# Two routed layers behind attention: the usual numbers of visits in line, wider first products, empty row groups not sent

## The chip, the cores and the metric

One core of one Trainium2 chip. The metric is the device time of one execution in microseconds (us), as the median of three runs. The engines are named as in the profile: PE (TensorE matmul) and PEld (its weight loads), DVE (VectorE), ACT (ScalarE), POOL (GpSimd), SP (SyncE, which issues most transfers).

## The reference

Attention with random features, then two layers with eight experts each. A token goes to the one expert with the largest logit; layer 0 keeps at most 576 tokens of an expert, layer 1 keeps all, and its logits have a bias that depends on the token's modality.

```python
# layer 0 (cap = 576); x: 2304 x 512, w1: 8 x 512 x 1024, w2: 8 x 1024 x 512
expert_idx = np.argmax(x @ w_gate, axis=1)
...
h = np.maximum(np.einsum('ecd,edf->ecf', disp, w1), 0.0)
y = np.einsum('ecf,efd->ecd', h, w2)
...
# layer 1
logits = x @ w_gate + modality_bias[modality_id]
e_idx = np.argmax(logits, axis=1)
...
    h = np.maximum(x[mask] @ w1[e], 0.0)
    out[mask] = gate_w[mask, None] * (h @ w2[e])
```

## The kernel before

The attention fills the first 255 us or so and isn't touched. Each layer is then worked off in visits. A visit takes up to 512 tokens of one expert, as four blocks of 128 rows:

- `fetch` (POOL) brings the rows `xrow` by four indirect DMAs; it is issued one or two visits ahead.
- `turn` transposes a block on PE (`pt<-ident,xrow`); ACT writes the upper part `xTh`, VectorE the rest `xTl`.
- `one` makes an eighth of the hidden layer: 12 matmuls (`pa<-xTh,wh`, `pa<-xTl,wh`, `pa<-xTh,wl`), with as many columns as the visit was built for; eight of them, 96 matmuls, make the first products.
- `keep` writes `hTh` (ACT) and `hTl` (VectorE). `piece` splits 512 columns of weights into `wh` (ACT) and `wl` (VectorE for the even pieces, POOL for the odd ones).
- `two` makes the second products, 24 matmuls for 128 columns or 128 tokens. In layer 1 it does so only for blocks below the built size.
- `out` (ACT) writes the result `y`. In layer 1 `put` (POOL) sends a block's rows to their places in the output by an indirect DMA, four in each visit, whether the block holds tokens or not; places outside the output are dropped.

Sizes are found at run time. `products` holds a matmul part once for each size in `BUILT`, and a nest of Ifs (L892) on PE alone takes one; they are called the arms. The number of visits is a run-time number as well. `others` and its inner `rest` write the program as a nest: visits 1 to 3 always run; then an If on the number of visits (L1221) holds one more full visit and the rest in its body, and the last visit in its Else. The bodies follow one another in line. All the Elses stand behind them, so that a layer's last visit is reached by a branch out of the line and left by another. (`final` is layer 0's last visit, which also fetches for layer 1; `last` is layer 1's.) Between the layers stands an If on the number of tokens of layer 1's first visit (L1258, L1259): with 512 of them `whole` runs, which mixes layer 0's last routing with layer 1's first visit; else a longer way. `L1.others` follows.

All of it is issued in written order on each engine: `in_order` ties each instruction to the one before it on its engine. Most rows of the profile therefore have the line of that helper, L55, or L53 for the first instruction of a block.

```python
                    with tc.If(self.visits > v + 1, preferred_fallthrough_block=True) as c:
                        self.visit(v)
                        rest(v + 1)
                    self.arm = arm
                    with c.Else():
                        self.visit(v, ("final", "last")[l])
```

Of the kernel before, what the change touches and what calls it, by code (L numbers as in the profile page):

```python
# [20 lines left out]
N, DM, E, FF = 2304, 512, 8, 1024  # L21
XW = 524
GATE, BIAS, TOK = 512, 513, 513
NV = 12
# [9 lines left out]
)  # L34

ALWAYS = (5, 5)


class InOrder:
# [21 lines left out]
def moe_chain_kernel(ctx, tc, q, k, v, w_phi, wg1, w1a, w2a, modality, wg2, mbias, w1b, w2b, out, cap):  # L61
    nc = tc.nc
    in_order = InOrder(tc)
# [726 lines left out]
    with ExitStack() as mo:  # L790
# [46 lines left out]
        class Layer:  # L837
# [69 lines left out]

            def one(self, f, n):

                ph = bank("pa", f)  # L910
                (xh, xl), (wh, wl) = xT, (t.rearrange("p f (c k) -> p f c k", c=4) for t in wgt[0])
                for m, (c, xt, wt) in enumerate((c, xt, wt) for c in range(4) for xt, wt in ((xh, wh), (xl, wh), (xh, wl))):
                    in_order.tensor.matmul(ph[:, 0:n], lhsT=wt[:, f, c, :], rhs=xt[:, c, 0:n], start=(m == 0), stop=(m == 11))
# [25 lines left out]
            def visit(self, v, kind=None):  # L939
# [71 lines left out]
                for f in range(4, 8):  # L1011
                    self.keep(f)
                    todo.pop(0)()
                self.mine(v, b)
                if kind is None and v + 2 < NV:
                    self.select(v + 2)
                if ev is not None:
# [4 lines left out]
                for c in range(2):  # L1022
                    for _ in range(2):
                        if later:
                            later.pop(0)()
                    self.out(c, b)
                    if l == 1:
                        self.put(c, b)
                for g in steps[2]:
                    g()  # L1030
                mine = self.arm
# [10 lines left out]
                for c in range(2, 4):  # L1042
                    for _ in range(2):
                        if later:
                            later.pop(0)()
                    self.out(c, b)
                    if l == 1:
                        self.put(c, b)
                for g in steps[3]:
                    g()  # L1050
                if kind in (None, "first") and v + 2 < (ALWAYS[0] if l == 0 else NV):
# [43 lines left out]
                self.fetch(2)  # L1095
                self.put(3, 0)

            def put(self, a, b):
                in_order.gpsimd.indirect_dma_start(out=out, out_offset=bass.IndirectOffsetOnAxis(ap=tokr[b][:, a, :], axis=0),
                                                   in_=y2[:, a, 0:DM], in_offset=None, bounds_check=N - 1, oob_is_err=False)  # L1100

# [106 lines left out]
                in_order.vector.tensor_scalar_add(first[l][:, 3:4], n, -1.0)  # L1208
                self.find_arm(0)

            def others(self):

                self.registers()
                l = self.l

                def rest(v):
                    if v + 1 == NV:
                        self.visit(v, ("final", "last")[l])
                        return
                    arm = self.arm  # L1220
                    with tc.If(self.visits > v + 1, preferred_fallthrough_block=True) as c:  # L1221
                        self.visit(v)
                        rest(v + 1)
                    self.arm = arm
                    with c.Else():
                        self.visit(v, ("final", "last")[l])

                if l == 1:
                    self.find_arm(1)
# [22 lines left out]
        L0.visit(0, "first")  # L1252
        i = 4 * NV + 1
        in_order.vector.tensor_scalar(out=lastv, in0=ctl[0][:, i - 1:i], scalar1=-1, scalar2=ALWAYS[0] - 1, op0=ALU.add, op1=ALU.max)
        L0.others()


        early = nc.values_load(first[1][0:1, 2:3], min_val=0, max_val=N)  # L1258
        with tc.If(early > 511) as c:  # L1259
            L1.whole()  # L1260
        with c.Else():
            for t in L0.tail():
                t()
            for f in visit_list(1, in_order.vector):
                f()
            L1.select(0)
            L1.fetch(0)
            L1.select(1)
            for a in range(4):
                L1.turn(a)  # L1270
            L1.fetch(1)
            L1.tokens()
            L1.visit(0)
        L1.others()


_INS = ["q", "k", "v", "w_phi", "moe_w_gate", "moe_w1", "moe_w2", "moe2_modality_id", "moe2_w_gate", "moe2_modality_bias", "moe2_w1", "moe2_w2"]
# [24 lines left out]
```

## Time and profile before

| what | us |
|---|---|
| runs | 887.31, 880.38, 880.18 |
| median | 880.38 |
| profiled execution, its own time | 886.04 |
| its span in the trace | 884.3 |
| PE busy in it | 783.4 |
| POOL busy in it | 434.5 |

In a row of the timeline the first number is the start from the span's begin, the second the duration, and the brackets say how long the engine had been idle and what ended that; `issue` means that it waited for nothing that the profile shows. Ends of matmuls are modelled, so the distance between starts tells their pace. In a row of the groups the number after x is the count, then busy time and mean ns of one, then the idle time before them. Numbers of buffers are left out of names.

### The profile page before, as it was taken

The page shows a single profiled execution, that of the slowest core. Times are in us where ns is not written, and L with a number is a line of the kernel's source. Part 1 is how long each engine was busy: PE and PEld are TensorE (multiplying, and loading weights), DVE is VectorE, ACT ScalarE, POOL GpSimd, SP SyncE. Part 2 cuts the span into 40 slices and gives each one's busy share as a digit, 9 for nine tenths or more (in the row PEclk, how much of TensorE's full clock was granted, in tenths as well). Part 3 has the DMA queues.
Part 4 walks back from the last instruction along what each step waited for, and adds up shares of the span by engine and source line. Part 5 has one row for each costly group of instructions (what it writes and reads, how often), then busy time and mean ns, then how long its engine had stood idle before and what let it go on. Part 6 is the DMA issues. An engine that isn't in the chain of part 4 may idle for free. (4 is left out here: it accounts for less than half of the span.)

```text
span 884.3 us, 15256 instructions
## 1 busy us (share of the span) xinstructions
PE 783.4 (89%) x5170; PEld 681.1 (77%) x5170; DVE 517.4 (59%) x1225; ACT 421.9 (48%) x807; POOL 434.5 (49%) x544
## 2 busy tenths in 40 slices
PE   7879999999939899999998886789699999998690
PEld 5649986589829789999988885767588888898590
DVE  7866687976647337477887765948232323266530
ACT  4547865578443335445545552522343434356431
POOL 4965537755242534564655633712644444466641
PEclk9999999999968999999999987999999999996755
DMA  8747623251032443537448444402762626274420
GB/s 268 249 174 264 211 75 112 63 215 60 3 98 92 150 171 119 200 108 269 156 141 290 140 153 142 154 2 99 236 221 83 206 66 224 72 237 139 132 52 6
DMA packets 70812, 129.44 MB, mean 146 GB/s; under 512 B 16388, under 2 KB 28804, under 8 KB 70660
## 3 DMA queue, kind: packets, MB, share of 16 engines
q1 hardware_dynamic: 60852, 103.33, 34.5%
q0 software_dynamic: 7360, 21.90, 8.6%
q10 hardware_dynamic: 2448, 2.20, 0.8%
q8 instruction: 92, 1.51, 0.7%
q14 instruction: 60, 0.49, 0.2%
HBM read 94.37 MB, written 35.67 MB: 147 GB/s over the span
## 5 line engine op out<-in xcount | busy, mean ns | idle before, releaser
L55 POOL TENSOR_TENSOR wl<-raw,wh 128x512 fp32r<-128x512 f32 x114 | 148.9, 1314 | 149.8 <-ACT wh L55 146.3
L55 PE MATMUL pa<-xTh,wl 128*128 128x512 f32 (+10 forms) x480 | 165.9, 346 | 1.7 <-issue 1.7
L55 PE MATMUL pa<-xTl,wh 128*128 128x512 f32 (+10 forms) x480 | 165.6, 345 | 0.1
L55 PE MATMUL pa<-xTh,wh 128*128 128x512 f32 (+10 forms) x451 | 155.8, 345 | 0.0
L55 ACT CAST wh<-raw 128x512 fp32r<-128x512 f32 x240 | 141.8, 620 | 6.1 <-DMA raw<-in_moe_w_dram 4.7
L55 DVE SCALAR_TENSOR_TENSOR hTl<-pa,hTh 128x512 fp32r<-128x512 f32 x112 | 76.8, 689 | 111.7 <-ACT hTh L55 110.9
L55 DVE TENSOR_TENSOR wl<-raw,wh 128x512 fp32r<-128x512 f32 x121 | 110.4, 921 | 46.3 <-ACT wh L55 46.3
L55 ACT ACTIVATE hTh<-pa 128x512 fp32r<-128x512 f32 x112 | 67.1, 599 | 138.8 <-PE pa L55 136.9
L55 PEld LDWEIGHTS pa<-xTh,wl 128*128 128x128 f32 x480 | 101.8, 212 | 7.3 <-issue 2.4
L55 PEld LDWEIGHTS pa<-xTl,wh 128*128 128x128 f32 x480 | 101.8, 212 | 5.7 <-DVE xTl L55 0.4
L55 PEld LDWEIGHTS pa<-xTh,wh 128*128 128x128 f32 x451 | 95.4, 212 | 4.6
L55 POOL DMA_INDIRECT xrow<-xs,rowi x61 | 64.8, 1062 | 51.9 <-DVE n L55 15.3
L55 PE MATMUL pa<-hTh,wl 128*128 128x424 f32 (+7 forms) x256 | 81.5, 318 | 4.4 <-POOL wl L55 4.4
L55 PE MATMUL pa<-hTl,wh 128*128 128x424 f32 (+7 forms) x256 | 81.3, 318 | 0.0
L55 PE MATMUL pa<-hTh,wh 128*128 128x424 f32 (+7 forms) x240 | 76.2, 318 | 0.0
L55 POOL DMA_INDIRECT out_dram<-y,tokr x28 | 28.3, 1011 | 75.5 <-ACT y L55 36.2
L541 PE MATMUL po<-kv,e 128*128 128x65 f32 x512 | 64.2, 274 | 0.5 <-DVE rank L677 0.5
L55 PE MATMUL pa<-wl,hTh 128*128 128x512 f32 x160 | 63.4, 396 | 0.6 <-DVE wl L55 0.6
L55 DVE TENSOR_TENSOR xTl<-pt,xTh 128x512 fp32r<-128x512 f32 x60 | 38.6, 681 | 42.7 <-ACT xTh L55 42.6
L55 PE MATMUL pa<-wh,hTl 128*128 128x512 f32 x160 | 63.2, 395 | 0.0
L541 PEld LDWEIGHTS po<-kv,e 128*128 128x128 f32 x512 | 61.0, 192 | 1.5 <-issue 0.8
L55 PE MATMUL pa<-wh,hTh 128*128 128x512 f32 x151 | 59.7, 395 | 0.0
(307 smaller groups left out, 1544.8 us busy)
## 6 DMA issues: line engine op xcount, KB each, us to landing
raw<-in_moe_w_dram SPq DMA_DIRECT2D x116, 512.0 KB, 5.1
xs<-hrow SPq DMA_DIRECT2D x18, 524.0 KB, 5.9
xs<-y SPq DMA_DIRECT2D x8, 1048.0 KB, 4.3
out_dram<-hrow SPq DMA_DIRECT2D x9, 512.0 KB, 4.7
qk_sb<-in_k_dram SPq DMA_DIRECT2D x16, 256.0 KB, 3.9
v_sb<-in_v_dram SPq DMA_DIRECT2D x16, 256.0 KB, 3.9
qk_sb<-in_q_dram SPq DMA_DIRECT2D x8, 512.0 KB, 3.8
xs<-y SPq DMA_DIRECT2D x2, 1024.0 KB, 5.5
```

The costliest lines, as they stand in the source:

```text
L55: return f(*a, **kw)
L541: nc.tensor.matmul(po[:, j, :], lhsT=e[:, sg, j, :], rhs=kv[:, h, it["b2"], sg, :], start=(sg == 0), stop=(sg == 1))
```

## The change

`LINE = (8, 7)` is new: for eight visits of layer 0 and seven of layer 1 the last visit stands in line. In `rest` the If at that visit is turned round: its body is the last visit, and more visits are in its Else. Layer 1 (`second`) is written into the body behind layer 0's eighth visit, and within it `L1.others` behind `whole`. Other numbers of layer 0's visits skip that and reach a second copy of layer 1 at the program's end. `one` takes at least 208 columns. A put of a block after the first is sent only if the visit has more tokens than stand in the blocks before; POOL reads that number once in a visit. The four puts in `whole` stay as they are.

```diff
+LINE = (8, 7)
...
             def one(self, f, n):
 
+                n = max(n, 208)
...
+                if l == 1:
+                    t = ctl[1][0:1, 2 * NV + v:2 * NV + v + 1] if v > 0 else first[1][0:1, 2:3]
+                    count = in_order.gpsimd.value_load(t, min_val=0, max_val=N)
...
                     if l == 1:
-                        self.put(c, b)
+                        self.put(c, b, count)
...
-            def put(self, a, b):
+            def put(self, a, b, count=None):
+
+                if count is not None and a > 0:
+                    with tc.If(count > 128 * a, preferred_fallthrough_block=True):
+                        self.put(a, b)
+                    return
...
-            def others(self):
+            def others(self, then=lambda: None):
...
+                def last(v):
+                    self.visit(v, ("final", "last")[l])
+                    if v + 1 == LINE[l]:
+                        then()
+
+                def more(v):
+                    self.visit(v)
+                    rest(v + 1)
+
                 def rest(v):
                     if v + 1 == NV:
-                        self.visit(v, ("final", "last")[l])
+                        last(v)
                         return
                     arm = self.arm
-                    with tc.If(self.visits > v + 1, preferred_fallthrough_block=True) as c:
-                        self.visit(v)
-                        rest(v + 1)
+                    if v + 1 == LINE[l]:
+                        cond, near, far = self.visits < v + 2, last, more
+                    else:
+                        cond, near, far = self.visits > v + 1, more, last
+                    with tc.If(cond, preferred_fallthrough_block=True) as c:
+                        near(v)
                     self.arm = arm
                     with c.Else():
-                        self.visit(v, ("final", "last")[l])
+                        far(v)
...
-        L0.others()
-
-
-        early = nc.values_load(first[1][0:1, 2:3], min_val=0, max_val=N)
-        with tc.If(early > 511) as c:
-            L1.whole()
...
+        def second():
+
+
+            early = nc.values_load(first[1][0:1, 2:3], min_val=0, max_val=N)
+            with tc.If(early > 511, preferred_fallthrough_block=True) as c:
+                L1.whole()
+                L1.others()
...
+                L1.others()
+
+        L0.others(second)
+        with tc.If(L0.visits != LINE[0], preferred_fallthrough_block=False):
+            second()
```

PE before, at the end of layer 0's last visit as the eighth, an Else: `pa` is the smallest arm of its second products, `pt` and `pm` are the transposes and a placing product behind them, L1221 is the If on the number of visits, and behind the branch stands another Else.

```order
L55 MATMUL pa_3497<-hTh,wl_3505 128x208
L892 UNCONDITIONAL_BRANCH
L55 MATMUL pt_3498<-ident,xrow 128x128 x4
L55 MATMUL pt_3499<-ident,xrow 128x128 x4
L55 MATMUL pt_3498<-ident,x 128x128 x4
L55 MATMUL pt_3499<-ident,x 128x128 x4
...
L55 MATMUL pm_3500<-B,A 128x320
L1221 UNCONDITIONAL_BRANCH
L892 COMPARE_AND_BRANCH
L53 MATMUL pa_3494<-xTh,wh_3502 128x512
```

PE in the changed program, at the end of the same visit: L1281 and L1282 are the If on layer 1's first visit, and `whole` begins with the 512-wide matmul.

```order
L57 MATMUL pa_3497<-hTh,wl_3505 128x208
L894 UNCONDITIONAL_BRANCH
L57 MATMUL pt_3498<-ident,xrow 128x128 x4
L57 MATMUL pt_3499<-ident,xrow 128x128 x4
L57 MATMUL pt_3498<-ident,x 128x128 x4
L57 MATMUL pt_3499<-ident,x 128x128 x4
...
L57 MATMUL pm_3500<-B,A 128x320
L1281 TENSOR_LOAD first_242
L1282 COMPARE_AND_BRANCH
L55 MATMUL pa_3494<-xTh,wh_3502 128x512
```

In the first, an unconditional branch leads away from the visit's end to the point where layer 1 begins; in the second, layer 1 begins behind the visit, with one compare between.

PE before, where `whole` ends: `pm_3501<-x,wgp` belongs to the Else of the If on layer 1's first visit.

```order
L55 MATMUL pa_3497<-wh_3504,hTl 128x512
L55 MATMUL pt_3498<-ident,xrow 128x128 x4
L55 MATMUL pt_3499<-ident,xrow 128x128 x4
L55 TENSOR_LOAD ctl_244
L55 ISA x2
L1259 UNCONDITIONAL_BRANCH
L53 MATMUL pm_3501<-x,wgp_226 32x512
```

PE in the changed program, at the same place.

```order
L57 MATMUL pa_3497<-wh_3504,hTl 128x512
L846 TENSOR_LOAD ctl_244
L57 TENSOR_LOAD ctl_244
L57 ISA x2
L57 MATMUL pt_3498<-ident,xrow 128x128 x4
L57 MATMUL pt_3499<-ident,xrow 128x128 x4
L57 TENSOR_LOAD ctl_244
L57 ISA x2
L894 COMPARE_AND_BRANCH
L55 MATMUL pa_3494<-xTh,wh_3502 128x512
```

The branch over the Else is gone, and the next visit's first products follow the compare of their arms.

POOL before, in a visit of layer 1: `out_dram<-y,tokr` are the puts, `xrow<-xs,rowi` the fetch of a later visit.

```order
L55 DMA out_dram<-y_254,tokr_3515 2304x512
L55 TENSOR_TENSOR wl_3503<-raw_247,wh_3502 128x512
L55 DMA out_dram<-y_254,tokr_3515 2304x512
L55 COPY side<-xrow 128x12 x2
L55 TENSOR_TENSOR wl_3503<-raw_247,wh_3502 128x512
L55 DMA out_dram<-y_254,tokr_3515 2304x512
L55 TENSOR_TENSOR wl_3503<-raw_247,wh_3502 128x512
L892 UNCONDITIONAL_BRANCH
L55 DMA out_dram<-y_254,tokr_3515 2304x512
L55 DMA xrow<-xs_61,rowi 128x524 x4
```

POOL in the changed program, in such a visit, from the second put on.

```order
L1107 COMPARE_AND_BRANCH
L55 DMA out_dram<-y_254,tokr_3515 2304x512
L1107 UNCONDITIONAL_BRANCH
L1107 ISA
L1107 UNCONDITIONAL_BRANCH
L57 COPY side<-xrow 128x12 x2
L57 TENSOR_TENSOR wl_3503<-raw_247,wh_3502 128x512
L1107 COMPARE_AND_BRANCH
L55 DMA out_dram<-y_254,tokr_3515 2304x512
L1107 UNCONDITIONAL_BRANCH
```

Each put but a visit's first now stands behind a compare, and both ways end in a branch.

## Rows read from the trace of the kernel before

**Rows 1.** Groups by line and shape, from 260 us on: visits, puts, and 128-column products

```profile
L55 DVE TENSOR_SCALAR groupr<-four_f 128x4 f32<-128x4 f32 x8 | 8.0, 996 | 0.0
...
L55 DVE CAST tokr<-sdr 128x4 int32<-128x4 f32 x7 | 3.3, 467 | 5.4 <-POOL sdr L55 5.4
...
L55 POOL DMA_INDIRECT out_dram<-y,tokr x28 | 28.3, 1011 | 75.5 <-ACT y L55 36.2 <-PEq L892 11.6 <-DMA out_dram<-y,tokr 11.3
...
L55 PE MATMUL pa<-xTh,wl 128*128 128x128 f32 x64 | 25.6, 399 | 0.0
```

**Rows 2.** Timeline of PE at the places out of line, and two starts of `pt`

```profile
538.89 0.54 PE L53 MATMUL pa<-xTh,wh 128*128 128x208 f32 x1 [6.09 <-issue]
...
577.21 0.47 PE L53 MATMUL pa<-xTh,wh 128*128 128x512 f32 x1 [3.13 <-issue]
...
579.45 0.79 PE L55 MATMUL pa<-xTh,wl 128*128 128x512 f32 x1 [0.84 <-issue]
...
637.51 0.78 PE L53 MATMUL pa<-xTh,wh 128*128 128x512 f32 x1 [5.66 <-issue]
...
817.74 2.25 PE L55 MATMUL pt<-ident,xrow 128*128 128x128 f32 x8 [0.89 <-DMA xrow<-xs,rowi]
...
826.03 1.03 PE L55 MATMUL pt<-ident,xrow 128*128 128x128 f32 x8
834.86 0.45 PE L53 MATMUL pa<-xTh,wh 128*128 128x128 f32 x1 [7.79 <-issue]
```

**Rows 3.** Timeline of PE at two starts in line

```profile
420.55 0.41 PE L53 MATMUL pa<-hTh,wh 128*128 128x320 f32 x1 [0.18 <-issue]
...
798.32 0.33 PE L53 MATMUL pa<-xTh,wh 128*128 128x128 f32 x1 [1.34 <-ACT wh L55]
```

**Rows 4.** Timeline of PE: ends of stretches whose pace is read off

```profile
544.98 0.28 PE L55 MATMUL pa<-xTl,wh 128*128 128x208 f32 x1
...
582.17 0.55 PE L55 MATMUL pa<-xTh,wl 128*128 128x512 f32 x1
...
640.23 0.53 PE L55 MATMUL pa<-xTh,wh 128*128 128x512 f32 x1
...
773.42 0.26 PE L53 MATMUL pa<-xTh,wh 128*128 128x208 f32 x1
...
784.13 1.04 PE L55 MATMUL pt<-ident,xrow 128*128 128x128 f32 x8
...
800.72 0.28 PE L55 MATMUL pa<-xTh,wh 128*128 128x128 f32 x1
...
855.37 0.73 PE L53 MATMUL pa<-wh,hTh 128*128 128x512 f32 x1
...
859.17 0.39 PE L55 MATMUL pa<-wh,hTh 128*128 128x512 f32 x1
...
862.34 0.39 PE L55 MATMUL pa<-wh,hTl 128*128 128x512 f32 x1
```

**Rows 5.** Windows: busy us by engine, granted clock of PE, DMA share, GB/s

```profile
774.00:784.00 10.00, 10.00 (x92) 10.00 (x91) 7.02 (x8) 8.00 (x15) 7.71 (x7) 1.00 0.88 281
...
802.00:810.00 8.00, 8.00 (x39) 8.00 (x39) 5.78 (x8) 5.69 (x12) 4.99 (x7) 0.50 0.03 7
```

**Rows 6.** Timeline of POOL: put 2 of the fifth visit, a piece, a fetch; the last puts

```profile
806.99 1.00 POOL L55 DMA_INDIRECT out_dram<-y,tokr  x1 [1.43 <-PE pa L55]
808.02 1.28 POOL L55 TENSOR_TENSOR wl<-raw,wh 128x512 fp32r<-128x512 f32 x1
...
811.16 1.04 POOL L55 DMA_INDIRECT xrow<-xs,rowi  x1 [0.30 <-issue]
...
863.87 1.05 POOL L55 DMA_INDIRECT out_dram<-y,tokr  x1 [5.64 <-ACT y L55]
...
873.40 0.97 POOL L55 DMA_INDIRECT out_dram<-y,tokr  x1 [1.86 <-DMA out_dram<-y,tokr]
```

**Rows 7.** Timeline of VectorE behind `whole`

```profile
632.13 1.29 DVE L55 TENSOR_TENSOR xTl<-pt,xTh 128x512 fp32r<-128x512 f32 x2 [1.89 <-ACT xTh L55]
```

More of the change, by code (lines that the diff above doesn't have):

```diff
@@ L1047, in visit @@
                     if l == 1:
-                        self.put(c, b)
+                        self.put(c, b, count)
                 for g in steps[3]:
@@ L1254, in moe_chain_kernel @@
         in_order.vector.tensor_scalar(out=lastv, in0=ctl[0][:, i - 1:i], scalar1=-1, scalar2=ALWAYS[0] - 1, op0=ALU.add, op1=ALU.max)
-        L0.others()
-        early = nc.values_load(first[1][0:1, 2:3], min_val=0, max_val=N)
-        with tc.If(early > 511) as c:
-            L1.whole()
[L1261 to L1274, printed above, removed]
+        def second():
[3 more added lines that the diff above has]
+                L1.others()
+            with c.Else():
+                for t in L0.tail():
+                    t()
+                for f in visit_list(1, in_order.vector):
+                    f()
+                L1.select(0)
+                L1.fetch(0)
+                L1.select(1)
+                for a in range(4):
+                    L1.turn(a)
+                L1.fetch(1)
+                L1.tokens()
+                L1.visit(0)
+                L1.others()
+        L0.others(second)
+        with tc.If(L0.visits != LINE[0], preferred_fallthrough_block=False):
+            second()
 _INS = ["q", "k", "v", "w_phi", "moe_w_gate", "moe_w1", "moe_w2", "moe2_modality_id", "moe2_w_gate", "moe2_modality_bias", "moe2_w1", "moe2_w2"]
```

## The prediction

> **What bounds the kernel now.** I read first how often things run, since the change is built on two counts. In the groups by line, `groupr<-four_f` runs once in each visit of layer 0: 8 times. `tokr<-sdr` runs once in each visit of layer 1: 7 times, and each of these makes four puts: 28 [rows 1]. So the visits are 8 and 7, the very numbers in `LINE`. The group of 128x128 first products holds 64 matmuls of one of three kinds; a visit has 32 of a kind, so two visits of layer 1 run 128 columns wide, and no other visit is under 208.
>
> Then TensorE (PE) in the timeline, from 260 us on, where the visits begin. It works nearly without a break but for the places where the program leaves the line. There the rows say `issue`: PE waited for no other engine and no transfer. There are four: 6.09 us before layer 0's last visit, 3.13 and again 0.84 us where layer 1's `whole` begins, 5.66 us after `whole`, and 7.79 us before layer 1's last visit [rows 2]. Where one visit or part follows another in line, the row shows 0.18 us `issue`, or a wait with another name, 1.34 us for a `wh` cast [rows 3]. After the long idles the clock is at the lower of its two levels (1.2 of 2.4 GHz): the 96 first products of the last visit take 20.51 us (834.86 to 855.37), 214 ns each, against 112 ns for the 96 of the fifth visit of layer 1 (773.42 to 784.13) [rows 2, 4]. The windows give the granted clock: 1.00 there, 0.50 in 802 to 810 us [rows 5].
>
> Last, POOL, which issues fetches and puts: in the final visit it puts four blocks one after the other with nothing else left to do, 863.87 to 873.40 us, and the span ends at 884.3 [rows 6]. So the end is set by PE up to 862.73 us (862.34 + 0.39), and by POOL's puts behind it.
>
> **The change part by part.** All terms are against the profiled execution, 886.04 us (span 884.3 and 1.74 around it).
>
> *Layer 0's last visit in line.* The idle of 6.09 us becomes one as in line, 0.2: 5.9. The cold stretch goes with it: 28 steps from 538.89 to 544.98 take 6.09 us; at 112 ns they take 3.1: 3.0 more [rows 2, 4]. PE then comes nearly 9 us earlier to second products whose lower weights POOL still has to make; I take off 0.9 for that. 8.0 (5 to 9).
>
> *Layer 1 behind it in line.* 3.13 + 0.84 - 0.2 = 3.8; the six steps from 579.45 to 582.17 take 2.72 us, and at 0.226 (14 steps from 859.17 to 862.34) 1.36: 1.4 more [rows 2, 4]. 5.1 (3.5 to 5.3).
>
> *Second visit of layer 1 behind `whole`.* Here the jump hides a wait: VectorE writes the last `xTl` until 633.42 us (632.13 + 1.29) [rows 7], so PE starts then and not at 631.9. 637.51 - 633.42 = 4.1, and six cold steps up to 640.23, 1.4 as before [rows 2, 4]. 5.4 (3.5 to 5.7).
>
> *Wide first products.* 128 columns become 208 in 2 x 96 matmuls. In `one` alone this costs nothing: at the upper clock 128 columns go at 114 ns (21 steps from 798.32 to 800.72), 208 at 112; at the lower one 208 columns go at 217 (28 steps, above), 128 at 214 [rows 3, 4]. The weight load is what a step waits for. What it may give is the clock. In the sixth visit 128 columns started at the upper level and the windows show 0.50 from 802 us on; in the last one they never rose, while the 208 columns of the fifth visit stayed at 1.00 and those of layer 0's last visit rose from the lower level after 6 us [rows 4, 5]. By the Trainium skill ("TensorE: Matmul & The Clock Gate", section "Back-to-back issue gap") a lone matmul's gap grows with its columns, N/2.4 + 2.5 ns at the upper clock; by that, 80 more columns in 192 matmuls would cost an estimated 6.4 us, and the sum would be 6.4 less. The rows (112 against 114 ns) do not bear it out for these pairs with a weight load each, so I leave it out.
>
> *Sixth visit.* Its `one` would end at about 809 us (798.32 + 96 x 0.112) instead of 816.9, but the transposes behind it wait for rows of the last visit, as now at 817.74 (0.89 for `xrow`) [rows 2]. These rows come from POOL's fetch, first at 811.16, which stands behind the puts 2 and 3 of the fifth visit. That visit has more than 128 tokens (it took the 208 arm) and at most 208, so those two puts go. Between 806.99 and 811.16 lie 4.2 us; one `wl` piece of 1.28 stays: 2.9; if the piece also moves into the 1.43 us that the put waited, 4.3 [rows 6]. I take 3.7 (1 to 5); the rest of the faster `one` is lost in that wait.
>
> *Last visit.* From the end of the sixth visit's second products (826.03) to PE's end (862.73) it is 36.7 us. In line it is 1.03 for the transposes, 1.34 as at the boundary before, 96 x 0.112 = 10.75 and 24 x 0.226 = 5.4: 18.5 [rows 2 to 4]. That is 18.2 less; POOL's pieces, which the jump had covered, get 0.7 of it back: 17.5 (13 to 18.2).
>
> *Puts not sent.* Two in the fifth visit, three in the sixth and seventh each (both had at most 128): 20 of 28 go out. Behind PE's end only put 0 is left: 873.40 - 863.87 = 9.5 us [rows 6]. Against that stand three skips and one more jump at the program's end on POOL; no row shows POOL skipping, so 0 to 4.5, and I take 1.5, three skips at PE's 0.2 and the rest for the jump. 8.0 (5 to 9.5).
>
> *What the Ifs cost.* Each put's If ends in a branch on every engine: three in a row on PE at the end of each of six visits, 18. By the in-line start with 0.18 us, where such a branch also stands [rows 3], at most 3.2; some hide behind the wait for `wh`. I take 1.0 (0 to 3.2). POOL also reads a count per visit; it waits 1.43 and 5.64 us ahead of two of its puts [rows 6], so nothing.
>
> The sum: 8.0 + 5.1 + 5.4 + 3.7 + 17.5 + 8.0 - 1.0 = 46.7. That makes 839.3 of 886.04. The median of the runs shown is 880.38, and the profiled run is like the slower of them (887.31); nothing in the change speaks to that difference, so 880.38 - 46.7 = **833.7 us**.
>
> **The rivals.**
>
> *A: the wide products don't hold the clock.* In the sixth and the last visit PE also waits (for rows, for the boundary), and after every idle of some microseconds the clock was low. Then the last visit's `one` stays at 20.5 (9.7 less gained), its second products start cold (1.8), and the sixth visit gains 0.9 instead of 3.7: 14.3 less, 848. For it: each long idle in rows 2 ends cold. Against it: the boundary is 1.34 us, after which the sixth visit began at full pace [rows 3, 4].
>
> *B: the idle is not the jump's.* If it came from what else stands at these places (loads of registers, the next weights), only the clock in the last visit (6.8: after 29 steps at 0.213, 67 at 0.112), second products (1.8), 3.7 and 8.0 remain, less 1.0 for the Ifs: 19.3, so 861. By the Trainium skill ("Advanced Engine Details and Errata", section "Control Flow Timing") a branch always taken costs about 51 ns and a compare with a branch 108; by this the jumps would be worth next to nothing. The rows with 5.66 to 7.79 us `issue`, and none in line over 0.2, speak against. The same skill ("Runtime: NRT & Kernel Launch", section "Instruction fetch mechanics") has a taken branch out of the fetched window wait for a transfer of instructions, which these rows fit.
>
> *C: the put Ifs jump, and it gets slower.* If each of PE's 18 branches cost what the shortest long jump does, 3.13 us [rows 2], that is 56 us on the path, 55 more than I took: 889, slower by 1.0%. It decides from 2.7 us (47.7 / 18) a branch. Against it: the targets stand right behind, and ends of arms with such branches show 0.18.
>
> *D: half of it.* The changed program holds layer 1 twice; if jumps within the arms get longer, or POOL's pieces become what PE waits for at each of the four places, about half of the 36 us at those places is kept, and the time is near 852.
>
> **How the numbers follow.** Forecast 0.72, A 0.13, D 0.08, B 0.04, C 0.03. About 1% is what a measurement of this kernel can tell from no change. All cases but C are faster by more than that; C, just at 1%, is halved. So faster 0.96, same 0.02, slower 0.02. The terms' lower ends together give 28 (852), their upper ends 53 (828), but all on one side is unlikely; with runs of one kernel 7 us apart, 824 to 849 holds the forecast and A.
>
> **What would show it.** In the profile after: PE's four `issue` idles under 0.5 us; 208-wide rows in two more visits, 112 ns apart, and granted clock 1.00 in the last visit; 20 puts; `xrow` named ahead of the sixth visit's transposes; one put behind PE's end and about 12 us from it to the end. Wrong: an `issue` of over 2 us at the beginning of any visit, or steps of 213 ns through the last visit (A), or idle with branches ahead of visits of layer 1 (C).

## The result, and the profile after

The changed kernel takes 851.19 us (median of 847.70, 850.30, 852.09 and 853.98) where the kernel before took 882.13 beside it: a ratio of 0.9638, 95% interval 0.9580 to 0.9697. In a second measurement it was 850.53 and 0.9606 (0.9548 to 0.9664). So it is faster, by 3.6 to 3.9%; I had forecast 5.3% (833.7 of 880.38), and the time lies outside my range of 824 to 849.

The profiled execution took 850.30 us, its span is 848.6. PE's timeline after the change, first at the places of [rows 2], then at the sixth and the last visit of layer 1 (the ordering helper is line L57 here, and L55 for the first instruction of a block):

```profile
530.57 0.70 PE L57 MATMUL pm<-B,A 128*128 128x320 bf16 x4 [1.41 <-POOL B L57]
...
531.36 0.36 PE L55 MATMUL pa<-xTh,wh 128*128 128x208 f32 x1
...
561.82 1.25 PE L57 MATMUL pt<-ident,x 128*128 128x128 f32 x8 [2.91 <-DVE xTl L57]
...
563.35 0.50 PE L55 MATMUL pa<-xTh,wh 128*128 128x512 f32 x1
...
580.21 0.24 PE L57 MATMUL pm<-ohb,ones_b 128*128 128x32 bf16 x4 [0.37 <-DVE ohb L57]
...
616.28 0.50 PE L55 MATMUL pa<-xTh,wh 128*128 128x512 f32 x1 [0.87 <-ACT xTh L57]
...
776.29 0.36 PE L55 MATMUL pa<-xTh,wh 128*128 128x208 f32 x1 [1.34 <-ACT wh L57]
...
786.10 0.54 PE L57 MATMUL pa<-xTh,wh 128*128 128x208 f32 x1 [2.35 <-DVE hTl L57]
...
794.33 0.66 PE L57 MATMUL pt<-ident,xrow 128*128 128x128 f32 x4 [0.36 <-DMA xrow<-xs,rowi]
...
800.67 1.03 PE L57 MATMUL pt<-ident,xrow 128*128 128x128 f32 x8
806.15 0.33 PE L55 MATMUL pa<-xTh,wh 128*128 128x208 f32 x1 [4.45 <-ACT y L57]
...
818.56 0.41 PE L55 MATMUL pa<-wh,hTh 128*128 128x512 f32 x1
...
823.82 0.39 PE L57 MATMUL pa<-wh,hTl 128*128 128x512 f32 x1
```

The idles of 6.09, 3.13 and 5.66 us are gone, or down to 0.87 behind `whole`, with `xTh` as what ends it. In place of 7.79 us before the last visit stand 4.45, put down to ACT's `y`. PE ends at 824.21 (823.82 + 0.39).

The windows of the same run (start and end, length, busy us of PE, PEld, VectorE, ACT and POOL with the number of instructions, then the granted clock, DMA share, GB/s):

```profile
786.00:794.00 8.00, 7.86 (x40) 7.62 (x40) 5.52 (x9) 2.65 (x5) 6.87 (x7) 0.58 1.00 342
...
806.00:810.00 4.00, 3.85 (x20) 3.88 (x21) 1.34 (x2) 2.59 (x5) 2.12 (x2) 0.57 0.03 10
810.00:818.00 8.00, 8.00 (x74) 8.00 (x73) 6.22 (x8) 6.14 (x13) 6.87 (x7) 1.00 0.57 124
```

The clock falls behind each of the idles of 2.35 and 4.45 us, but comes back: in the last visit it is at its upper level from 810 us on, where it was 0.50 throughout before.

POOL's timeline, the answer to [rows 6], with the header that gives the span:

```profile
core 0 of [0], span 848.6 us
...
781.07 1.02 POOL L55 DMA_INDIRECT out_dram<-y,tokr  x1 [3.47 <-ACT y L57]
...
786.19 1.06 POOL L57 DMA_INDIRECT xrow<-xs,rowi  x1 [1.30 <-DVE hTl L57]
...
825.35 1.05 POOL L57 DMA_INDIRECT out_dram<-y,tokr  x1 [3.47 <-DVEq L1301]
```

Put 0 of the last visit is the last row of POOL, as forecast. But from its start to the end of the span it is not 12 us, it is 23.3 (848.6 - 825.35), and no view names anything in that stretch. Before, all four puts and the end took 20.4 (884.3 - 863.87).

The table cuts both profiles at the same instructions, term by term. Of the cuts in the profile before, these three are not in the rows above the prediction:

```profile
532.09 0.70 PE L55 MATMUL pm<-B,A 128*128 128x320 bf16 x4 [1.41 <-POOL B L55]
...
572.28 1.25 PE L55 MATMUL pt<-ident,x 128*128 128x128 f32 x8 [1.83 <-DVE xTl L55]
...
596.60 0.24 PE L55 MATMUL pm<-ohb,ones_b 128*128 128x32 bf16 x4 [0.38 <-DVE ohb L55]
```

| stretch, before and after | before | after | gain | forecast |
|---|---|---|---|---|
| up to the last `pm` of layer 0's seventh visit | 532.09 | 530.57 | 1.5 | 0 |
| layer 0's last visit, up to its `pt<-ident,x` at 572.28 and 561.82 | 40.2 | 31.3 | 8.9 | 8.0 |
| `whole` begins, up to the `pm<-ohb` at 596.60 and 580.21 | 24.3 | 18.4 | 5.9 | 5.1 |
| up to the sixth visit of layer 1 (798.32 and 776.29) | 201.7 | 196.1 | 5.6 | 5.4 |
| sixth visit (to 826.03 and 800.67) | 27.7 | 24.4 | 3.3 | 3.7 |
| last visit (to 862.73 and 824.21) | 36.7 | 23.5 | 13.2 | 17.5 |
| from PE's end to the span's end | 21.6 | 24.4 | -2.8 | 8.0 |
| what the Ifs cost on PE | | | in the rows above | -1.0 |
| sum | | | 35.7 | 46.7 |

Up to the last visit the forecast holds within 1 us a term. It fails in two: the last visit (4.3 us) and the end (10.8 us).

### The profile page after: what moved, and what is told of

Read it like the earlier page. It is cut to its first block, busy times and chain, and to the rows that moved or that the text cites. A ratio compares the mean times of both kernels' runs of the same rounds, so it can differ in the third digit from the quotient of the medians.

```text
span 848.6 us, 15272 instructions
## 1 busy us (share of the span) xinstructions
PE 758.8 (89%) x5170; PEld 657.9 (78%) x5170; DVE 519.2 (61%) x1225; ACT 422.1 (50%) x807; POOL 426.7 (50%) x536
## 3 DMA queue, kind: packets, MB, share of 16 engines
q8 instruction: 86, 1.41, 0.7%
## 5 line engine op out<-in xcount | busy, mean ns | idle before, releaser
L57 POOL TENSOR_TENSOR wl<-raw,wh 128x512 fp32r<-128x512 f32 x114 | 148.6, 1311 | 133.9 <-ACT wh L57 127.0
L57 PE MATMUL pa<-xTl,wh 128*128 128x208 f32 (+9 forms) x480 | 157.0, 327 | 0.7 <-issue 0.4
L57 PE MATMUL pa<-xTh,wl 128*128 128x208 f32 (+9 forms) x480 | 156.7, 327 | 0.0
L57 PE MATMUL pa<-xTh,wh 128*128 128x208 f32 (+9 forms) x451 | 147.9, 328 | 2.4 <-DVE hTl L57 2.4
L57 ACT CAST wh<-raw 128x512 fp32r<-128x512 f32 x240 | 142.0, 621 | 7.3 <-DMA raw<-in_moe_w_dram 5.0
L57 DVE TENSOR_TENSOR wl<-raw,wh 128x512 fp32r<-128x512 f32 x121 | 113.4, 946 | 45.5 <-ACT wh L57 45.3
L57 DVE SCALAR_TENSOR_TENSOR hTl<-pa,hTh 128x512 fp32r<-128x512 f32 x112 | 76.6, 688 | 90.9 <-ACT hTh L57 90.1
L57 ACT ACTIVATE hTh<-pa 128x512 fp32r<-128x512 f32 x112 | 67.3, 601 | 120.0 <-PE pa L57 120.0
L57 PEld LDWEIGHTS pa<-xTl,wh 128*128 128x128 f32 x480 | 93.5, 195 | 6.2 <-DVE xTl L57 1.1
L57 PEld LDWEIGHTS pa<-xTh,wl 128*128 128x128 f32 x480 | 93.5, 195 | 4.7
L57 PEld LDWEIGHTS pa<-xTh,wh 128*128 128x128 f32 x451 | 87.9, 195 | 7.2 <-DVE hTl L57 2.5
L57 POOL DMA_INDIRECT xrow<-xs,rowi x61 | 63.6, 1043 | 53.3 <-DVE rowi L57 19.0
L57 PE MATMUL pa<-hTh,wl 128*128 128x424 f32 (+7 forms) x256 | 80.2, 313 | 2.6 <-POOL wl L57 2.6
L57 PE MATMUL pa<-hTl,wh 128*128 128x424 f32 (+7 forms) x256 | 79.9, 312 | 0.0
L57 PE MATMUL pa<-hTh,wh 128*128 128x424 f32 (+7 forms) x240 | 75.0, 312 | 0.0
L57 DVE TENSOR_TENSOR xTl<-pt,xTh 128x512 fp32r<-128x512 f32 x60 | 38.6, 681 | 42.7 <-ACT xTh L57 42.6
L57 PE MATMUL pa<-wl,hTh 128*128 128x512 f32 x160 | 62.4, 390 | 0.6 <-DVE wl L57 0.6
L57 PE MATMUL pa<-wh,hTl 128*128 128x512 f32 x160 | 62.4, 390 | 0.0
L57 PE MATMUL pa<-wh,hTh 128*128 128x512 f32 x151 | 59.0, 391 | 0.0
L477 POOL TENSOR_TENSOR u<-e 128x512 f32<-128x512 f32 x32 | 41.8, 1329 | 32.2 <-ACT e L457 29.0
```

What stands on the lines that cost most here:

```text
L57: return f(*a, **kw)
L477: nc.gpsimd.tensor_tensor(out=u, in0=e[:, :, 4 * b2:4 * b2 + 2, :], in1=e[:, :, 4 * b2 + 2:4 * b2 + 4, :], op=ALU.add)
```

## The experiments

For each run the table has two numbers of its profile beside its time: PE's stretch from the last `pm` of layer 0's seventh visit to PE's end (the start of the last matmul + 0.39), and the end, from there to the end of the span. The first leaves out what differs between executions ahead of that point.

| run | median us | ratio to before | PE's stretch | end |
|---|---|---|---|---|
| before (its first profile) | 882.13 | 1 | 330.6 | 21.6 |
| changed | 851.19 | 0.9638 (0.9580 to 0.9697) | 293.6 | 24.4 |
| e5_changed_again | 850.53 | 0.9606 (0.9548 to 0.9664) | 295.2 | 24.5 |
| e1_puts_all | 866.28 | 0.9789 (0.9764 to 0.9815) | 301.5 | 31.3 |
| e2_last_one_put | 846.39 | 0.9540 (0.9501 to 0.9580) | 297.9 | 18.9 |
| e3_narrow | 859.46 | 0.9722 (0.9681 to 0.9763) | 305.6 | 24.7 |
| e4_jump | 865.46 | 0.9762 (0.9711 to 0.9813) | 315.0 | 19.4 |
| e6_no_copy | 845.05 | 0.9521 (0.9486 to 0.9557) | 295.8 | 19.6 |
| e7_two_one_out | 847.79 | 0.9584 (0.9533 to 0.9635) | 295.6 | 19.1 |
| e8_one_if | 865.16 | 0.9757 (0.9717 to 0.9796) | 309.0 | 22.0 |
| e9_one_size | 843.29 | 0.9502 (0.9444 to 0.9559) | 292.9 | 20.8 |
| e10_one_size_end | 836.72 | 0.9456 (0.9409 to 0.9502) | 291.7 | 14.0 |
| e11_last_one_if | 849.50 | 0.9583 (0.9537 to 0.9630) | 293.4 | 21.4 |
| e12_line_only | 872.18 | 0.9816 (0.9749 to 0.9884) | 305.7 | 31.2 |
| e13_arms_last | 851.36 | 0.9607 (0.9542 to 0.9673) | 293.1 | 25.2 |
| e14_arms_all | 840.69 | 0.9482 (0.9421 to 0.9543) | 291.2 | 25.2 |
| e15_arms_one_if | 837.02 | 0.9439 (0.9376 to 0.9501) | 293.4 | 20.9 |

Runs e1 to e4, e5 to e8, e9 to e12 and e13 to e15 each share a chip and the runs of before; a ratio is taken against those. The changed kernel's own two profiles differ by 1.6 us in PE's stretch, so less than about 2 us there tells nothing.

**e5: the changed kernel once more,** with no edit, beside e6 to e8.

> The changed kernel as it is, beside the next three, for a comparison on one chip: ratio to the kernel before 0.958 to 0.970 as measured, 23.3 us from POOL's last put to the span's end.

As expected; 23.35 us from put to end.

**e1: all puts sent.** Theory 1 was that the way round a put is no cheaper than the put (in the order of the changed kernel it holds an ISA row); theory 2 that a put not sent is free. POOL's reading of the count goes too.

```diff
-                if l == 1:
-                    t = ctl[1][0:1, 2 * NV + v:2 * NV + v + 1] if v > 0 else first[1][0:1, 2:3]
-                    count = in_order.gpsimd.value_load(t, min_val=0, max_val=N)
+                count = None
...
             def put(self, a, b, count=None):
 
-                if count is not None and a > 0:
-                    with tc.If(count > 128 * a, preferred_fallthrough_block=True):
-                        self.put(a, b)
-                    return
```

> The changed kernel with all four puts of every visit sent again, in line and wide as it is. Theory 1 (the way round a put is no cheaper than the put: its ISA row holds POOL about 2 us): behind PE's end four puts take 9.5 us as before, and the end with its extra jump some 15, together 24.7 against 24.4 now; the fetch for the last visit is 2 to 4 us later; 849 to 855 us, no change that can be told. Theory 2 (a put not sent is free, and the long end comes from elsewhere): the three puts add 9.5 us at the end, 858 to 863.

PE's timeline, then POOL's:

```profile
791.60 1.12 PE L57 MATMUL pt<-ident,xrow 128*128 128x128 f32 x4 [5.62 <-DMA xrow<-xs,rowi]
```

```profile
core 0 of [0], span 857.6 us
...
827.48 1.05 POOL L57 DMA_INDIRECT out_dram<-y,tokr  x1 [3.77 <-ACT y L57]
...
839.14 0.98 POOL L57 DMA_INDIRECT out_dram<-y,tokr  x1 [2.15 <-DMA out_dram<-y,tokr]
```

Slower by 1.6 to 1.9% than the changed kernel (by the ratios), and 866.28 us is above what either theory gave. Theory 1 as I wrote it falls: leaving the puts out is worth 7.9 us on PE's stretch, 6.3 against the second profile (the wait for the last visit's rows is 5.62 us; with the Ifs 0.36, and 2.1 in e5), and 6.9 at the end. But theory 2 has the wrong size too. From put 0 to put 3 it is 11.7 us here; with 6.9 gained, the three skips keep some 5. And behind the last put stand 18.5 us (857.6 - 839.14), where [rows 6] had 10.9. So the long end has at least two parts, and e2 and e6 weigh one each.

**e2: the last visit without Ifs.**

```diff
+                self.few = l == 1 and kind == "last" and v == 6
...
+                if count is not None and a > 0 and self.few:
+                    return
```

> The changed kernel, whose last visit of layer 1 (the seventh) emits only put 0, without the three Ifs; blocks 1 to 3 of that visit are left out of the program (these inputs have no tokens in them). Theory 1: three times some 2 us go from the end, 6 us, so 844 to 846 by the profile of now (850.3), and from POOL's put to the span's end 17 instead of 23.3 us. Theory 2: no change, 850.

```profile
core 0 of [0], span 848.3 us
...
830.59 1.05 POOL L57 DMA_INDIRECT out_dram<-y,tokr  x1 [3.96 <-ACT y L57]
```

17.7 us from the put to the end, 5.6 less than 23.3: on the average each put that isn't sent costs 1.8 to 1.9 us there. The rest of theory 1 stands for the end. The time follows (0.954), though the profiled run lost 3 to 4 us on PE, with 5.32 us idle before the last visit.

Where POOL has other work between the skips, less of them shows. In the sixth visit of the changed kernel the skips of puts 1, 2 and 3 stand ahead of these three rows of POOL:

```profile
804.76 0.32 POOL L57 COPY side<-xrow 128x12 f32<-128x12 f32 x2 [0.43 <-issue]
...
807.40 1.27 POOL L57 TENSOR_TENSOR wl<-raw,wh 128x512 fp32r<-128x512 f32 x1 [0.55 <-DMA out_dram<-y,tokr]
...
810.19 1.07 POOL L57 DMA_INDIRECT xrow<-xs,rowi  x1 [1.52 <-DMA out_dram<-y,tokr]
```

That is 2.5 us of idle for three skips; in e7, which has neither the skips nor the `y` of these blocks, it is 0.15.

**e6: no second copy behind the main line.**

```diff
         L0.others(second)
-        with tc.If(L0.visits != LINE[0], preferred_fallthrough_block=False):
-            second()
```

> The changed kernel without the second copy of layer 1 and its If at the program's end; left out are the other numbers of visits of layer 0, which these inputs don't have. Theory E (the end is long because POOL takes two long jumps there, one over the Elses and one over the copy, with a row of its own for the If): some 4 to 5 us of the 23.3 between POOL's put and the end go, 18 to 19 left, 845.5 against 850 for the changed kernel. Rival (one jump over everything costs what two cost, or the end waits for the put's landing): under 1.5 us.

```profile
core 0 of [0], span 846.7 us
...
828.23 1.05 POOL L57 DMA_INDIRECT out_dram<-y,tokr  x1 [2.56 <-ACT y L57]
```

18.5 us from put to end, 4.9 less than the 23.35 of the changed kernel beside it (848.7 - 825.35). Theory E holds. Most of the end is accounted for with that: of 9.5 us for three puts, 5.6 stay as skips; leaving the line over the copy costs 4.9; some 2 more are left between 18.5 - 5.6 = 12.9 here and 10.9 before, which no run takes apart (e12, which has no put Ifs, has them too: 873.8 - 855.46 - 4.9 = 13.4). The sum is 9.5 - 5.6 - 4.9 - 2.0 = -3.0, against -2.8 measured.

**e3: 128 columns again.**

```diff
             def one(self, f, n):
 
-                n = max(n, 208)
```

> The changed kernel with first products of 128 columns again. Theory W (width holds the clock, as I forecast): the last visit's 96 first products take 20 us instead of 12.4 at the lower clock, the sixth visit's 18.5 instead of 17.1; 8 to 9 us slower, 858 to 860. Rival: in line, with shorter waits, 128 columns stay at the upper clock too, under 2 us difference, 850 to 852.

```profile
804.00:814.00 10.00, 9.98 (x48) 10.00 (x49) 4.72 (x7) 5.38 (x10) 6.99 (x7) 0.51 0.28 60
814.00:824.00 10.00, 10.00 (x49) 10.00 (x48) 5.46 (x7) 4.42 (x8) 3.57 (x3) 0.50 0.31 56
```

These are windows of the last visit's first products: the lower clock to their end. It is 0.9 to 1.2% slower than the changed kernel, and PE's stretch is 12 us longer (10 against the second profile); theory W holds, a little above its size. Rival A falls: with 128 columns the clock stays down, with 208 it rises within 4 us of the start.

**e4: the counts taken out of line.**

```diff
-LINE = (8, 7)
+LINE = (9, 8)
```

> The changed kernel with LINE = (9, 8), so that eight and seven visits take the way out of line at all places; wide and with the put Ifs. Theory J (the four idles are the jumps'): the idles of 3 to 8 us are back at the last visit of layer 0, between the layers and at the last visit of layer 1, and 20 to 26 us of the gain are lost: 870 to 877. Rival B of the prediction (the idle comes from what else stands there): under 4 us of loss, 850 to 854.

```profile
536.72 0.54 PE L55 MATMUL pa<-xTh,wh 128*128 128x208 f32 x1 [6.47 <-issue]
...
574.79 0.77 PE L55 MATMUL pa<-xTh,wh 128*128 128x512 f32 x1 [2.23 <-issue]
...
630.21 0.50 PE L55 MATMUL pa<-xTh,wh 128*128 128x512 f32 x1 [0.87 <-ACT xTh L57]
...
824.99 0.51 PE L55 MATMUL pa<-xTh,wh 128*128 128x208 f32 x1 [7.75 <-issue]
```

The `issue` idles come back where this run jumps, and stay away behind `whole`, which here too is followed in line: rival B falls. PE's stretch is 20 to 21 us longer. The time is only 1.2 to 1.6% longer, under what I had expected, because the end is 5 us shorter: layer 1 runs as the second copy here, which is the last code of the program, so nothing is jumped over at the end.

**e12: the line alone.** The edits of e1 and e3 together:

```diff
-                n = max(n, 208)
...
+                count = None
...
-                if count is not None and a > 0:
-                    with tc.If(count > 128 * a, preferred_fallthrough_block=True):
-                        self.put(a, b)
-                    return
```

> The kernel before with the visits in line alone: 128 columns and all puts. If the parts add, with 14.7 us for the puts and 12.2 for the width by the profiles of the two runs that undo one of them, less some 3 since both are partly spent on the wait for the last visit's rows: 872 to 877, a ratio of 0.985 to 0.992. If the line is worth what the four idles and their cold stretches say (some 25 us on PE less 5 at the end), 862 to 867.

```profile
core 0 of [0], span 873.8 us
...
843.75 1.05 POOL L57 DMA_INDIRECT out_dram<-y,tokr  x1 [5.74 <-ACT y L57]
...
855.46 0.98 POOL L57 DMA_INDIRECT out_dram<-y,tokr  x1 [2.12 <-DMA out_dram<-y,tokr]
```

872.18 us lies in the first expectation; the ratio of 0.9816 is a little under the range that I gave, which its interval reaches. So the parts add about as they should. The line takes 25 us off PE's stretch (330.6 to 305.7) and gives 9.6 back at the end (21.6 to 31.2); alone it is worth 1.8% (1.2 to 2.5). The width and the puts bring the other half of the gain.

**e7, e9 and e13: the idle before the last visit.** The trace puts 4.45 us down to ACT's `y`, and I believed it: with one block in a visit PE is through with the second products early, and ACT has four `y` and eight casts to do.

```diff
             def out(self, c, b):
+                if self.few and c > 0:
+                    return
...
+                self.few = l == 1 and v in (5, 6)
...
+                if count is not None and a > 0 and self.few:
+                    return
```

> The changed kernel, whose sixth and seventh visits of layer 1 work out and put block 0 alone: no y for blocks 1 to 3 on ACT, no puts and no Ifs for them; these blocks are left out of the program (these inputs have no tokens in them). Theory A (the 4.45 us idle before the last visit is ACT's row of y and wh, which the jump had covered before): three y of 0.6 us less, the idle falls to 2.4 to 2.9, the last visit begins at the upper clock sooner; with the 5.5 us of the skips at the end 7 to 9 us in all, 841 to 843. Rival (the idle is set by the wh casts or by xTl, not by y): the idle stays over 4, only 5.5 us go, 844.5.

```profile
805.53 0.33 PE L55 MATMUL pa<-xTh,wh 128*128 128x208 f32 x1 [4.33 <-ACT wh L57]
```

Theory A falls: the `y` are gone, the idle is there, under another name. What is left at that place is a branch: the arms of a visit are a nest, the 512-wide one follows the compare, the smallest is in the last Else. One size in `BUILT` for these two visits takes the branch away:

```diff
-    [(512, 448, 256)] * 3 + [(512, 464, 256), (512, 208, 128)] + [(512, 256, 128)] * 7,
+    [(512, 448, 256)] * 3 + [(512, 464, 256), (512, 208, 128)] + [(128,)] * 2 + [(512, 256, 128)] * 5,
```

> The run with block 0 alone in the sixth and seventh visits of layer 1, and in these two visits just one built size, 128, so that PE has no branch to an arm there; left out are other sizes of these visits and blocks 1 to 3. Theory R (the 4.3 us idle before the last visit are PE's branch to the smallest arm; the wh and y that the trace names were over before): the idle falls to 3 us or less, with xTl as what ends it, PE ends 1.5 to 3 us earlier than with block 0 alone (295.6 us behind the last pm of layer 0's seventh visit then). Rival (ACT's casts end it): the idle stays at 4.2 or more.

```profile
800.46 1.03 PE L57 MATMUL pt<-ident,xrow 128*128 128x128 f32 x8
801.63 0.33 PE L55 MATMUL pa<-xTh,wh 128*128 128x208 f32 x1
```

No idle at all, and none at this place in e10, which has the same edit. Theory R holds, and `xTl` doesn't take its place, as I had thought it would. Part of the gain goes to waits for `hTl` in the visit; PE ends 2.7 us earlier than in e7. e13 leaves nothing out and puts the smallest arm into the If's body instead:

```diff
+                def usual():
+                    n = len(sizes)
+                    with tc.If(self.arm > n - 2, preferred_fallthrough_block=True) as c:
+                        f(sizes[n - 1])
+                    with c.Else():
+                        among(0, n - 1)
...
-                    among(0, len(sizes))
+                    if self.l == 1 and v >= 5:
+                        usual()
+                    else:
+                        among(0, len(sizes))
```

> The changed kernel with the smallest arm in line in the sixth and later visits of layer 1, the other sizes in the Else; nothing is left out. Theory R (the 4.2 to 4.5 us idle before the last visit is PE's branch to that arm): the idle falls under 0.6 us; some of it comes back as waits for hTl within the visit, PE ends about 292.5 us behind the last pm of layer 0's seventh visit (293.6 and 295.2 in the two profiles of the changed kernel), 847 to 849 by the profile. Rival (the gain of the run with one size came from the blocks and sizes left out): idle over 3.5 us, no earlier end.

```profile
805.79 0.33 PE L55 MATMUL pa<-xTh,wh 128*128 128x208 f32 x1 [1.86 <-ACT y L57]
...
819.10 0.50 PE L57 MATMUL pa<-wl,hTh 128*128 128x512 f32 x1 [1.41 <-POOL wl L55]
```

The idle falls to 1.86 us, not under 0.6, and 1.41 us come new as a wait for POOL's `wl`: no gain in the time. By itself the 1.86 shows little, since with the branch in place the same idle differs from run to run: 4.45 and 4.21 us in the two profiles of the changed kernel, 5.32 in e2, 3.99 in e8 and e11, but 2.61 in e1, and in e6

```profile
808.44 0.33 PE L55 MATMUL pa<-xTh,wh 128*128 128x208 f32 x1 [1.92 <-ACT y L57]
```

That the branch makes most of it rests on e9 and e10 against e7; the 1.85 and 1.04 of e14 and e15, with the same edit, fit. Where the rest comes from is open. It isn't the `y` that the trace names: in e15 PE starts at 795.15, before the same `y` ends (795.03 + 0.69).

**e14: the smallest arm in line in layer 0 too.** These inputs take the smallest arm in each visit of layer 0, at 32 starts of a part (four in each of eight visits). At 24 of them the changed kernel shows no idle of PE, so most of these branches cost it nothing that can be seen. Four have idles that the trace puts down to VectorE's routing rows:

```profile
378.22 0.43 PE L55 MATMUL pa<-hTh,wh 128*128 128x360 f32 x1 [2.81 <-DVE eq L57]
...
449.88 0.39 PE L55 MATMUL pa<-hTh,wh 128*128 128x280 f32 x1 [1.27 <-DVE rowi L57]
...
483.23 0.38 PE L55 MATMUL pa<-hTh,wh 128*128 128x240 f32 x1 [2.42 <-DVE sh L57]
...
514.61 0.37 PE L55 MATMUL pa<-hTh,wh 128*128 128x224 f32 x1 [1.75 <-DVE lg L57]
```

The edit is e13's with a wider condition (against e13):

```diff
-                    if self.l == 1 and v >= 5:
+                    if self.l == 0 or v >= 5:
```

> The same, and the smallest arm in line in all visits of layer 0 too, where these inputs take it each time. Theory R2 (in layer 0 the idles of PE at the first product of a part that the trace puts down to VectorE's eq, sh, lg and rowi, 8.2 us in the changed kernel's profile, are branches to the smallest arm): these names go from PE's waits, together under 2 us are left, 5 to 8 us less on PE, 840 to 844. Rival (PE does wait for VectorE there): the idles stay, 847 to 849.

```profile
481.35 0.37 PE L55 MATMUL pa<-hTh,wh 128*128 128x240 f32 x1 [0.50 <-issue]
...
513.35 0.36 PE L55 MATMUL pa<-hTh,wh 128*128 128x224 f32 x1 [0.54 <-issue]
```

The rows at 378 and 450 have no idle of 0.3 us any more, the other two have 0.5. From the first product of layer 0's first visit to the last `pm` of its seventh it is 256.4 us (265.52 to 521.96) instead of 263.3 (267.31 to 530.57) in the changed kernel. Theory R2 holds; a matmul of `hTh` and `wh` reads neither `eq` nor `sh`, so those names were only those of rows that ended about then.

**e8, e11 and e15: one If for three puts.** One If around puts 1 to 3 has one ISA row on its way round instead of three. In every visit:

```diff
-                if count is not None and a > 0:
-                    with tc.If(count > 128 * a, preferred_fallthrough_block=True):
-                        self.put(a, b)
+                if count is not None and a == 1:
+                    self.held = True
+                    return
+                if count is not None and a == 2:
+                    return
+                if count is not None and a == 3:
+                    with tc.If(count > 128, preferred_fallthrough_block=True):
+                        for i in (1, 2, 3):
+                            self.put(i, b)
                     return
```

> The changed kernel with one If a visit around puts 1 to 3 (sent if there are over 128 tokens), and those puts after all four y: two ISA rows fewer on the way round, two more puts in the fifth visit. Nothing is left out. Theory 1 (1.85 us for each skip): from POOL's put to the end 19.6 us instead of 23.3; the fetch behind the fifth visit's puts 1 to 3 us later, which the sixth visit's transposes wait for; 1 to 3 us faster than the changed kernel, 847 to 849. Rival (the one ISA row takes as long as three, since it waits for three transfers): no change at the end, 850 to 853.

```profile
809.78 1.12 PE L57 MATMUL pt<-ident,xrow 128*128 128x128 f32 x4 [9.35 <-DMA xrow<-xs,rowi]
```

Theory 1 gets the direction of the end right and not the size: from put to end it is 20.9 us against 23.35, 2.5 less and not 3.7. The price lay elsewhere: the fifth visit now sends puts 1 to 3 behind its last `y`, the fetch comes later, and PE waits 9.35 us for `xrow` in the sixth visit. The run is 1.6% slower than the changed kernel beside it. In the last visit alone (e11):

```diff
+                self.final = kind == "last"
...
+                if count is not None and a > 0 and self.final:
+                    if a == 3:
+                        with tc.If(count > 128, preferred_fallthrough_block=True):
+                            for i in (1, 2, 3):
+                                self.put(i, b)
+                    return
```

> The changed kernel with one If around puts 1 to 3 in the last visit alone; nothing is left out. Theory 1: 20.9 us from POOL's put to the end instead of 23.3, as in the run with one If everywhere, and nothing else, since the fetches of other visits stay where they were: 847.5 to 848.5 where the changed kernel has 850.4. Rival (the one If costs the other visits elsewhere): PE's end moves by over 2 us.

20.3 us from put to end, 3.0 less, and nothing elsewhere; the time (0.9583 against 0.9606) can't tell it from none, the profile can. Against the 17.7 of e2 the one skip that is left costs 2.6 us, so three skips cost less than three times one.

The edits of e9 and e6 together make e10:

> The same without the second copy of layer 1 at the program's end (as left out before). If the terms add: 13 us from POOL's put to the end (23.3 less 5.4 for three skips and 4.9 for the copy's jump), and the earlier end of PE: a profiled run of 837 to 840, where the changed kernel has 850.4; a ratio of 0.944 to 0.950. If the parts only move a wait: over 843.

e10 adds up what the runs before took apart: 12.9 us from put to end (833.8 - 820.91) and 835.51 by its profile, somewhat under the expectation; PE's stretch is the shortest but one too.

Those of e14 and e11 together make e15:

> The same with one If around puts 1 to 3 in the last visit; nothing is left out. If the parts add: 2.5 to 3 us less than the run with the arms alone, all of it between POOL's put and the end (20.3 instead of 23.3 us); 838 to 841, ratio 0.946 to 0.951. Else as the run before.

e15 leaves nothing out: the smallest arms and the last visits in line, and one If for the last visit's puts. 837.02 us, 0.9439 (0.9376 to 0.9501), a little under what I had expected: from put to end it is 19.7 us, 4.3 less than in e14, while PE's stretch is 2.2 longer. It is faster than the kernel before by 5.6%, and its interval lies under that of the changed kernel.

## Why the prediction was right and wrong

- *The visits are 8 and 7, and the idle is the jump's.* Right. The idles went with the line and came back in e4 where the counts leave it. The terms for layer 0's last visit, for `whole` and for the visit behind it were within 1 us. In part that is luck: the 0.9 that I took off layer 0's last visit for POOL's weights shows as no such wait, and the wait for `xTl` grew by 1.1 instead (1.83 to 2.91). The 1.0 for the Ifs on PE shows in no row: from 618 us on PE has no idle put down to `issue`.
- *The wide products.* Right in both halves: 208 columns go at 111 ns (8 steps from 531.56 to 532.45), as 128 do at the upper clock, and the clock comes back with them. Without them PE's stretch is 10 to 12 us longer (e3). The growth with the columns that the prediction weighs for lone matmuls does not show in these.
- *The sixth visit.* 3.3 of 3.7, by the step that I gave: the wait for `xrow` falls when the two puts ahead of the fetch go (0.36 us with the Ifs, 2.1 in e5, 5.62 with all puts in e1, whose sixth visit takes 28.35 us, 772.34 to 800.69, where the changed kernel's takes 24.4). A wait of 2.35 us for `hTl` and a fall of the clock behind it came new, and the faster `one` had room for them.
- *The last visit* is mis-sized, 13.2 instead of 17.5. The failed step: "1.34 as at the boundary before". The idle is 4.45 us; that is 3.1 of the miss, and 1.7 more come because the products start at the lower clock behind it (12.4 us for 96 instead of 10.75); the 0.7 that I had taken off for POOL's pieces was not needed. At the last visit PE takes a branch to the smallest arm. At the boundary before it takes one too, and that one costs little: 1.34 us there, 0.68 with the arm in line (e13). So one branch was no measure for the other, and why the second is dearer no run shows. I had priced the jumps that the change removes, and not asked which jumps PE still makes; e9 and e14 show that there were more, covered by names of other engines.
- *The end* is the larger miss, 8.0 forecast, -2.8 measured. The failed step: "three skips at PE's 0.2 and the rest for the jump", 1.5 us in all. The skips take 5.6 (e2), leaving the line over the copy 4.9 (e6), and 2.0 are left open. The order of the changed kernel had shown an ISA row on the way round each put, and I took it for a branch; my bound of 4.5 us came from no row, and it should have been as long as the nearest row, a put with its wait, which is 3.2 us each.
- *The base.* I took 46.7 us, worked out against a profiled run of 886.04, from a median of 880.38. Later runs of the kernel before have medians of 882.1 to 886.7, so its usual time is nearer to the profiled one. That moves the forecast by 2 to 6 us, beside the 15 that the two terms were off.
- Rival A falls with e3, B with e4. C, a branch at each put that slows PE, has no row; yet the put Ifs do cost something, not on PE where I looked, but on POOL at the end. D's 852 is near to the time measured. It names jumps within the arms, and one of those is what the last visit pays for; but D has it at all four places and says nothing of the end, so that its number fits is chance, and so is that of A's 848.

## What to carry to other kernels

When a jump is taken out, look for the next one: an idle before the first instruction of an arm or a block may be a branch though the profile names an engine, and the test is to turn the arm that is taken into the line. For layer 0 that gave 10.7 us (840.69 in e14 against 851.36 in e13; by the two profiles 9.6 of them fall between layer 0's first product and PE's end). A transfer that is skipped at run time is not free on the engine that would have sent it: read in the order of the program what stands on the other way, and price it before it goes to where nothing covers it. And code that is kept for other counts should not stand behind the usual path, where jumping over it is the last thing the program does.

## What the runs showed of the hardware that was not expected

In the last visit a put that is not sent costs about 1.85 us on the average (5.6 for three, e2), nearly twice the 1.0 us of the put itself, with no row in the profile; where POOL has work between them three skips leave it idle for 2.5 us, and one skip alone costs 2.6 (e11 against e2). A way out of the line over unused code at the end cost 4.9 us (e6). The Trainium skill ("Runtime: NRT & Kernel Launch", section "Instruction fetch mechanics") says that a taken branch to code outside the fetched pages waits until that page is brought in; idles of 1.3 to 7.8 us at the branches of e4, of e7 and of the changed kernel in layer 0 agree with it, and so does that most branches to a smallest arm there cost PE nothing; that instructions were being fetched in these idles no row shows. Idles of one and the same branch differ between programs: before the last visit 4.45 and 4.21 us in the changed kernel's two profiles, 4.33 in e7 and 5.32 in e2, but 1.92 in e6; why e6 pays less was not tried.
